# Gated linear attention with a multiplicative FFN: natural feature order, PSUM banks shared 4 + 2, and TensorE in a written order from unit 1 on

## The chip, the cores and the metric

The kernel runs on one core of one Trainium2 chip. The metric is device microseconds for one execution. The engines are TensorE (PE, with its weight loads PEld), VectorE (DVE), ScalarE (ACT), GpSimd (POOL) and SyncE (SP, which issues the DMAs here). All of the work is in float32.

## The reference, cut to what matters

```python
# q, k, v, a_re, a_im: (4 batches, 8 heads, 768 steps, 48)
mag = np.sqrt(a_re * a_re + a_im * a_im)
scale = np.minimum(mag, 0.999) / (mag + 1e-06)
a_re_n, a_im_n = (a_re * scale, a_im * scale)
for t in range(S):                       # complex state S_re, S_im: (B, H, 48, 48)
    new_re = ar * S_re - ai * S_im
    new_im = ar * S_im + ai * S_re
    kv = np.einsum('bhd,bhe->bhde', k[:, :, t], v[:, :, t])
    S_re, S_im = (new_re + kv, new_im)
    y[:, :, t] = np.einsum('bhd,bhde->bhe', q[:, :, t], S_re)
x = y as (3072 tokens, 384 features)
a = x @ w1                               # 384 x 1024
b = x @ w2                               # 384 x 1024
h = a * b @ w3                           # 1024 x 1024
return h @ w_out                         # 1024 x 384
```

## The kernel before, in words

The sequence is cut into 8 units: unit u is one half (384 steps) of one batch, even u the first half and odd u the second. A unit has three chunks of 128 steps. Each unit goes through three parts.

`gates(u)` (L456) works on time-last tiles of 128 x 3 x 384. It turns the gates into running products inside a chunk (gA, L508) and running angles (gZ, L533), and from them into cosine and sine parts of q and k. It is a chain of some fifteen steps, on ScalarE (logarithm, exponential, arctangent, sine, all through L469), VectorE (scans and products, L489 to L554) and GpSimd (three products, L484, L520, L521). Its last steps copy the results by DMA into KL and QL (L563), 96 rows per head. Two sets of these buffers exist (`sides[0]`, `sides[1]`), for even and odd units, so a unit's gates take the buffers that the unit two before it used. `spread_v` (L440), called in it, lays v out into 64 columns per head for the matmuls.

The attention of a chunk has four kinds of matmul. `tp` (L578) transposes the gated k, whose two parts are gR and k, and ScalarE copies it to KT (L579). `sc` (L583) makes the scores of four heads into a bank, and VectorE copies them into A under the causal mask (L584). `y` (L601 to L612) adds V by A and, but for a batch's first chunk, the state T by QL; four column groups of 32 work beside each other, and ScalarE copies the result to xT (L614). `kv` (L619) makes the state's increment, which VectorE adds and scales into T (L625, L626). The last chunk of an odd unit needs no transposes and no state.

The FFN of a unit has eight groups `ffn_ab` (six matmuls m into two banks, L636, then a copy on ScalarE, L640, and a product on VectorE, L641) and three output tiles `ffn_out` (eight matmuls o each, L646; a copy, L649; a store, L651). w3 by w_out is multiplied beforehand, in `fuse` (f, L718).

The weights come as 64-bit floats. `convert` (L659) loads the raw words and turns them into float32 with two ScalarE steps (L670, L671) and four VectorE steps (L672, L674, L675, L676). w1 and w2 are 384 x 1024; each is converted in three tiles of 128 rows.

The features of x stand in an order of their own. Rows 0 to 127 are the first 32 features of heads 0 to 3, rows 128 to 255 the same of heads 4 to 7, rows 256 to 383 the last 16 of all heads. So w1 and w2 are loaded by pieces: four loads of 32 rows for each of the first two tiles, eight loads of 16 rows for the third.

PSUM has eight banks here: two for scores (`ps_s`), one each for tp, y and kv (`ps_1`), three for m, o and f (`ps_m`).

The order of the work is made by a scheduler. The program writes the steps of a unit's attention and of the FFN of the unit before interleaved (`interleave`, L770), with one step of the next unit's gates behind each. From this order as priority and from a cost model the scheduler then makes a fixed stream for each engine: what is ready by its model goes first. On the chip each engine runs its stream in order. `general` (L21) is a fallback that does not run with these inputs; `judge` (L721) decides that by one small matmul near the end.

Of the kernel before, what the change touches and what calls it, by code (L numbers as in the profile page):

```python
# [10 lines left out]
FP = mybir.dt.float32  # L11
# [9 lines left out]
def general(ctx, tc, qt, kt, v, art, ait, w1s, w2s, w3o, ident, out):  # L21
# [83 lines left out]
    def attention(u):  # L105
# [148 lines left out]
        for g in range(2):  # L254
            hd = 2 * hp + g
            for f0, d0, d1 in ((P * (hd // 4) + 32 * (hd % 4), 0, 32), (2 * P + 16 * hd, 32, D)):
                nc.scalar.copy(out=xn_t[b][:, :, f0:f0 + d1 - d0], in_=ys[:, g, :, d0:d1])
# [58 lines left out]
def kernel(  # L316
# [36 lines left out]

# [32 lines left out]
    ps_1 = fast.enter_context(tc.tile_pool(name="ps_1", bufs=1, space=PSUM))  # L386
    ps_m = fast.enter_context(tc.tile_pool(name="ps_m", bufs=3, space=PSUM))
# [26 lines left out]
    g_t, L_t, xT_t, ab_t, T_t, y_t = {}, {}, {}, {}, {}, {}  # L414
# [13 lines left out]
    def load_qkv(u):  # L428
# [6 lines left out]

        vr = one.tile([P, UC, DM], FP, tag="vr", name="vr")
# [131 lines left out]
    def scores(u, c):  # L568
        QL, KL, R, K2 = L_t[u]
        last = u % 2 and c == UC - 1  # L570
        w = slice(c * C, (c + 1) * C)
        A = Ab[(u * UC + c) % 2]
        KT = None if last else two.tile([P, H, 2, D], FP, tag="KT", name="KT")
        for x, src in enumerate((R, K2)):
            if not last:
                tp = ps_1.tile([P, KD, C], FP, tag="tr", name="tp")
                for f in range(KD):
                    nc.tensor.transpose(out=tp[:, f], in_=src[:, f, w], identity=ident)  # L578
                nc.scalar.copy(out=KT[:, :, x], in_=tp.rearrange("p f c -> p (f c)").rearrange("p (d h) -> p h d", h=H))  # L579
            sc = ps_s.tile([P, H // 2, C], FP, tag="sc", name="sc")  # L580
            for j in range(H // 2):
                hd = x * H // 2 + j
                nc.tensor.matmul(out=sc[:, j], lhsT=KL[:, hd, w], rhs=QL[:, hd, w], start=True, stop=True)  # L583
# [248 lines left out]
```

## Time and profile before

| | |
|---|---|
| median of the runs | 711.06 us (704.51, 711.06, 712.73) |
| profiled execution: time | 713.92 us |
| profiled execution: span from first to last instruction | 712.1 us |
| mean granted clock of TensorE | 0.933 |
| busy: TensorE, VectorE, ScalarE, GpSimd | 589.1, 358.4, 256.4, 109.5 us |
| scores of units 1 to 7 begin at | 222.3, 293.2, 367.8, 442.6, 512.5, 587.2, 646.6 us |

In what follows, a row of a timeline has the start, the length, the engine, the line, the operation with its output and inputs, the shape, and in brackets how long the engine had been idle before it and what ended that. Successive instructions of a kind are merged, with their count; one float32 matmul of the program is two instructions. TensorE's busy time counts a matmul from its start to its modelled end, so that a wait between pipelined matmuls can be hidden in it. The clock row of the page has the share of full speed that was granted, in tenths.

### The profile page before, as it was taken

Reading aid. Unit: us, or ns where it says so; the run is one execution under the profiler, and the core shown is the slowest. Engines: PE = TensorE matmul, PEld = TensorE weight load, DVE = VectorE, ACT = ScalarE, POOL = GpSimd, SP = SyncE. Lnnn points to the kernel's source line nnn. Section 1 sums busy time; section 2 is a strip of 40 time slices with the busy share of each in tenths; the row PEclk is TensorE's granted clock in tenths of the full one; section 3 lists DMA queues with packets and bytes.
Section 4 is the critical chain, followed back from the end, with each engine's and each line's share of the span. In section 5 each row is a group of like instructions: output and inputs, shape, how many; then the busy total and the mean of one; then the engine's idle time right before and its main releaser. Section 6 shows DMA issues by size and latency. Waiting matters only on the chain.

```text
span 712.1 us, 8939 instructions
## 1 busy us (share of the span) xinstructions
PE 589.1 (83%) x3514; PEld 382.9 (54%) x3514; DVE 358.4 (50%) x509; ACT 256.4 (36%) x362; POOL 109.5 (15%) x113
## 2 busy tenths in 40 slices
PE   0087994688907899979989899999899999999996
PEld 0044572244506656745667466755675657667553
DVE  2999828667675582358116830774068503103110
ACT  6664514454745533154044502551345101100110
POOL 4355001012122311121012100320122000000000
PEclk9998997699956999999989999999889999999999
DMA  8896975721979504943009700690092009200001
GB/s 238 274 284 191 177 162 124 154 67 33 108 136 115 110 0 114 123 98 100 0 25 123 188 0 1 93 212 30 0 131 37 12 0 117 41 12 13 13 0 37
DMA packets 45044, 65.77 MB, mean 92 GB/s; under 512 B 4288, under 2 KB 43200, under 8 KB 44224
## 3 DMA queue, kind: packets, MB, share of 16 engines
q1 hardware_dynamic: 44992, 65.10, 46.7%
q8 instruction: 29, 0.48, 0.3%
q14 instruction: 23, 0.19, 0.1%
HBM read 41.42 MB, written 4.72 MB: 65 GB/s over the span
## 4 chain that ended last, share of the span: by engine, by line
PE 55%; DVE 20%; ACT 10%; issue 8%; DMA 4%; SPq 2%; DVEq 0%; ACTq 0%
PE m L636 19%; PE o L646 16%; PE sc L583 7%; PE f L718 4%; PE kv L619 3%; DVE gZ L533 3%; DVE gA L508 2%; PE tp L578 2%; ACT gR L469 2%; ACT gZ L469 2%; DMA q<-in_q_dram 2%; DMA raw<-in_w_dram 2%; DVE cf L675 2%; PE y L601 2%; ACT KT L579 2%
## 5 line engine op out<-in xcount | busy, mean ns | idle before, releaser
L636 PE MATMUL m<-xT,w1s 128*128 128x384 f32 x384 | 143.9, 511 | 17.4 <-DVE w1s L676 10.0
L636 PE MATMUL m<-xT,w2s 128*128 128x384 f32 x384 | 138.2, 496 | 9.8 <-DVE w2s L676 8.6
L646 PE MATMUL o<-w3o,ab 128*128 128x384 f32 x384 | 129.7, 494 | 2.7 <-DVE ab L641 2.7
L636 PEld LDWEIGHTS m<-xT,w1s 128*128 128x128 f32 x384 | 73.3, 197 | 73.4 <-DVE w1s L676 12.6
L636 PEld LDWEIGHTS m<-xT,w2s 128*128 128x128 f32 x384 | 73.9, 194 | 65.5 <-DVE w2s L676 11.0
L584 DVE COPY_PREDICATED A<-causal,sc 128x512 f32<-128x512 int32 x48 | 35.1, 739 | 143.4 <-PE sc L583 143.2
L646 PEld LDWEIGHTS o<-w3o,ab 128*128 128x128 f32 x384 | 72.3, 192 | 50.9 <-DVE ab L641 3.3
L718 PE MATMUL f<-wo_s,w3s 128*128 128x384 f32 x128 | 47.9, 538 | 42.9 <-DVE w3s L676 42.9
L641 DVE TENSOR_TENSOR ab<-m,a 128x384 f32<-128x384 f32 x64 | 35.3, 551 | 94.3 <-PE m L636 91.4
L640 ACT COPY a<-m 128x384 f32<-128x384 f32 x64 | 30.3, 474 | 121.2 <-PE m L636 119.6
L718 PEld LDWEIGHTS f<-wo_s,w3s 128*128 128x128 f32 x128 | 26.7, 212 | 62.2 <-DVE w3s L676 43.5
L583 PE MATMUL sc<-QL,KL 96*128 96x128 f32 x384 | 57.6, 317 | 0.0
L583 PEld LDWEIGHTS sc<-QL,KL 96*128 96x128 f32 x384 | 55.0, 229 | 2.9 <-issue 0.8
L484 POOL TENSOR_TENSOR im<-im,gR 128x1152 f32<-128x1152 f32 (+1 forms) x10 | 20.3, 2041 | 229.6 <-ACT gR L469 194.2
L579 ACT COPY KT<-tp 128x384 f32<-128x384 f32 x40 | 19.2, 479 | 95.9 <-PE tp L578 95.5
L614 ACT COPY xT<-y 128x384 f32<-128x384 f32 x24 | 11.4, 475 | 78.5 <-PE y L612 48.8
L520 POOL TENSOR_TENSOR q<-q,gA 128x1152 f32<-128x1152 f32 (+1 forms) x10 | 28.5, 2847 | 61.4 <-DVE gA L508 48.5
L619 PEld LDWEIGHTS kv<-V,KT 128*96 128x96 f32 x320 | 30.1, 165 | 6.1 <-issue 4.4
L578 PE MATMUL tp<-ident,gR 128*128 128x128 f32 x60 | 12.2, 313 | 25.2 <-DVE gR L549 19.6
L619 PE MATMUL kv<-V,KT 128*96 128x64 f32 x320 | 30.8, 248 | 0.9 <-DVE T L625 0.9
L670 ACT ACTIVATE low<-raw 128x1024 int32<-128x1024 uint32 (+1 forms) x18 | 19.7, 1095 | 22.5 <-DVE cf L675 18.4
L521 POOL TENSOR_TENSOR k<-k,gR 128x1152 f32<-128x1152 f32 (+1 forms) x10 | 23.3, 2341 | 23.5 <-DVE gR L518 23.5
(88 smaller groups left out, 670.3 us busy)
## 6 DMA issues: line engine op xcount, KB each, us to landing
raw<-in_w_dram SPq DMA_DIRECT2D x8, 1024.0 KB, 6.0
KL<-gR SPq DMA_DIRECT2D x24, 193.5 KB, 5.1
KL<-k SPq DMA_DIRECT2D x24, 193.5 KB, 7.9
re<-in_a_re_dram SPq DMA_DIRECT2D x24, 192.0 KB, 9.8
im<-in_a_im_dram SPq DMA_DIRECT2D x24, 192.0 KB, 6.5
k<-in_k_dram SPq DMA_DIRECT2D x24, 192.0 KB, 5.3
q<-in_q_dram SPq DMA_DIRECT2D x24, 192.0 KB, 5.0
vr<-in_v_dram SPq DMA_DIRECT2D x8, 576.0 KB, 5.9
```

Source lines behind the costliest of these rows:

```text
L469: chain(nc.scalar.activation(**kw))
L520: nc.gpsimd.tensor_tensor(out=q[:, s], in0=q[:, s], in1=A[:, s], op=OP.mult)
L578: nc.tensor.transpose(out=tp[:, f], in_=src[:, f, w], identity=ident)
L579: nc.scalar.copy(out=KT[:, :, x], in_=tp.rearrange("p f c -> p (f c)").rearrange("p (d h) -> p h d", h=H))
L583: nc.tensor.matmul(out=sc[:, j], lhsT=KL[:, hd, w], rhs=QL[:, hd, w], start=True, stop=True)
L584: nc.vector.copy_predicated(out=A[:, x * H // 2:(x + 1) * H // 2], data=sc, mask=causal.rearrange("p (h t) -> p h t", h=1).to_broadcast([P ...
L619: nc.tensor.matmul(out=kv[:, hd], lhsT=KT[:, hd], rhs=V[:, hd], start=True, stop=True)
L636: nc.tensor.matmul(out=m, lhsT=w[:, f, j * P:(j + 1) * P], rhs=xT_t[u][:, f], start=(f == 0), stop=(f == KD - 1))
L640: nc.scalar.copy(out=a, in_=got[0])
L641: nc.vector.tensor_tensor(out=ab_t[u][:, j], in0=got[1], in1=a, op=OP.mult)
L646: nc.tensor.matmul(out=m, lhsT=ab_t[u][:, f, t * P:(t + 1) * P], rhs=w3o[:, f], start=(f == 0), stop=(f == KF - 1))
L718: nc.tensor.matmul(out=m, lhsT=w3_t[j][:, f], rhs=wo_s[:, f], start=(f == 0), stop=(f == KF - 1))
```

## The change: what it does

Five things are changed at once. The features of x get their natural order (head by head), so w1 and w2 are loaded in three whole tiles each, six loads in place of 32. v is spread by two GpSimd copies per unit in place of nine; of the heads' 64 columns the odd heads now use the last 48. The twelve blocks of 32 features that y is made of are spread over the four column groups as `QUADS`, and the products with V and with T follow each other per block. tp, y and kv share two banks (`ps_v`), and the FFN gets four. And `scores`, `outputs` are cut into `turn`, `scores`, `outputs` and `state`, whose order against the FFN groups is written out in `pieces` and `unit`; from unit 1 on TensorE's stream is exactly that order (`manual_schedule`), while the other engines are still placed by the scheduler.

```diff
-    ps_1 = fast.enter_context(tc.tile_pool(name="ps_1", bufs=1, space=PSUM))
-    ps_m = fast.enter_context(tc.tile_pool(name="ps_m", bufs=3, space=PSUM))
+    ps_v = fast.enter_context(tc.tile_pool(name="ps_v", bufs=2, space=PSUM))
+    ps_m = fast.enter_context(tc.tile_pool(name="ps_m", bufs=4, space=PSUM))
...
-        for c in range(UC):
-            nc.gpsimd.tensor_copy(out=V[:, c, :, 0, 0:D], in_=vr[:, c, :, 0])
-            nc.gpsimd.tensor_copy(out=V[:, c, :, 1, 0:LO], in_=vr[:, c, :, 1, 0:LO])
-            nc.gpsimd.tensor_copy(out=V[:, c, :, 1, D:D + HI], in_=vr[:, c, :, 1, LO:D])
+        for i, e0 in enumerate((0, 64 - D)):
+            nc.gpsimd.tensor_copy(out=V[:, :, :, i, e0:e0 + D], in_=vr[:, :, :, i])
...
+    QUADS = [q for h in range(0, H, 2) for q in ([(h, 0)], [(h, 1), (h + 1, 0)], [(h + 1, 1)])]
...
+        y = ps_v.tile([P, KD, C], FP, tag="v", name="y")
+        lanes = [[] for _ in range(4)]
+        for i, q in enumerate(QUADS):
+            f, j = divmod(i, 4)
+            o = y[32 * j:32 * j + 32, f]
+            got = [(V[:, hd, 32 * e:32 * e + 32], A[:, hd]) for hd, e in q]
+            if not first:
+                got += [(T[:, hd, 32 * e:32 * e + 32], QL[:, hd, w]) for hd, e in q]
+            lanes[j] += [(o, a, b, n == 0, n == len(got) - 1) for n, (a, b) in enumerate(got)]
+        for step in zip(*lanes):
+            for o, a, b, s0, s1 in step:
+                nc.tensor.matmul(out=o, lhsT=a, rhs=b, start=s0, stop=s1)
...
-        got = []
-        for d, w in ((w1s, w1), (w2s, w2)):
-            hs = words(w).rearrange("(h x e) m -> h e x m", x=1, e=D)
-            for f, (h0, h1, e0, e1) in enumerate(((0, 4, 0, LO), (4, 8, 0, LO), (0, H, LO, D))):
-                srcs = [hs[hd, e0:e1] for hd in range(h0, h1)]
-                got.append(lambda d=d, f=f, srcs=srcs: load_weight(d[:, f:f + 1], srcs))
-        return got
+        return [lambda d=d, f=f, src=words(w).rearrange("(f p) m -> p f m", p=P): load_weight(d[:, f:f + 1], src[:, f:f + 1])
+                for d, w in ((w1s, w1), (w2s, w2)) for f in range(KD)]
...
+    def pieces(u):
+
+        sc = [[lambda c=c, x=x: scores(u, c, x) for x in range(2)] for c in range(UC)]
+        tr = [[lambda c=c, x=x: turn(u, c, x) for x in range(2)] for c in range(UC)]
+        kv = [lambda c=c: state(u, c) for c in range(UC)]
+        y = [lambda c=c: outputs(u, c) for c in range(UC)]
+        got = [[tr[0][0]], [tr[0][1]], sc[0], [tr[1][0], kv[0]], [tr[1][1], y[0]], sc[1] + [tr[2][0]], [kv[1], tr[2][1]],
+               [y[1]] + sc[2], [kv[2]], [y[2]]]
+        if u % 2:
+            got[5], got[6], got[8] = sc[1], [kv[1]], []
+        return got
...
+    def unit(u):
         steps = gates(u + 1, False) if u + 1 < NU else iter(())
-        for f in interleave(att, ffn(u - 1) if u else []):
-            f()
-            next(steps, None)
+        rest = ffn(u - 1) if u else []
+        for i, p in enumerate(pieces(u)):
+            for f in rest[i:i + 1] + p:
+                f()
+                next(steps, None)
+        for f in rest[len(pieces(u)):]:
+            f()
+            next(steps, None)
         for _ in steps:
             pass
...
+    unit(0)
+    with tc.manual_schedule(engines={mybir.EngineType.PE}):
+        for u in range(1, NU):
+            unit(u)
+        judge()
+        for f in ffn(NU - 1):
+            f()
```

What the engines' streams make of it is shown at three places. A row there has the line, the operation, the output and inputs with the tile's own number behind the name, the shape and a count. Lines of the changed kernel are its own.

TensorE before, from the FFN of unit 1 into the attention of unit 2 (ab_1294 and o are of FFN(1), sc and y of unit 2):

```order
L646 MATMUL o_1595<-w3o_60,ab_1294 128x384 x8
L646 MATMUL o_1631<-w3o_60,ab_1294 128x384 x8
L619 MATMUL kv_1677<-V0_87,KT_1492 96x64 x8
L646 MATMUL o_1689<-w3o_60,ab_1294 128x384 x7
L583 MATMUL sc_1328<-QL_1215,KL_1214 128x128 x4
L583 MATMUL sc_1339<-QL_1215,KL_1214 128x128 x4
L583 MATMUL sc_1378<-QL_1215,KL_1214 128x128 x4
L583 MATMUL sc_1389<-QL_1215,KL_1214 128x128 x4
L601 MATMUL y_1434<-A0_85,V0_87 32x128 x8
L608 MATMUL y_1434<-A0_85,V0_87 32x128 x8
L583 MATMUL sc_1498<-QL_1215,KL_1214 128x128 x4
```

TensorE now, at the start of unit 3 (m is of FFN(2); tp, sc and kv are of unit 3):

```order
L634 MATMUL m_1650<-xT_1408,w1s_58 128x384 x3
L634 MATMUL m_1654<-xT_1408,w2s_59 128x384 x3
L571 MATMUL tp_1678<-ident_61,gR_1262 128x128 x3
L634 MATMUL m_1686<-xT_1408,w1s_58 128x384 x3
L634 MATMUL m_1690<-xT_1408,w2s_59 128x384 x3
L571 MATMUL tp_1698<-ident_61,k_871 128x128 x3
L634 MATMUL m_1704<-xT_1408,w1s_58 128x384 x3
L634 MATMUL m_1708<-xT_1408,w2s_59 128x384 x3
L581 MATMUL sc_1718<-QL_1443,KL_1442 128x128 x4
L581 MATMUL sc_1735<-QL_1443,KL_1442 128x128 x4
L634 MATMUL m_1743<-xT_1408,w1s_58 128x384 x3
L634 MATMUL m_1747<-xT_1408,w2s_59 128x384 x3
```

The attention stood in one block behind the FFN of the unit before, its pieces behind each other; now each piece has an FFN group before and behind it.

VectorE before, where the gates of unit 1 end (gR_635, k_602), and the rows up to the first masks of unit 1 begin with the gates of unit 2 (gZ_907):

```order
L641 TENSOR_TENSOR ab_893<-m_1142,a_1146 128x384
L549 TENSOR_TENSOR gR_635<-k_602,re_341 128x3x384
L553 TENSOR_TENSOR gA_634<-q_601,re_341 128x1152
L550 TENSOR_TENSOR k_602<-k_602,gZ_636 128x3x384
L554 TENSOR_TENSOR q_601<-q_601,gZ_636 128x1152
L625 TENSOR_TENSOR T_1076<-kv_1067,T_823 96x512
L489 ISA gZ_907,st_tan_98<-im_445 128x1152
```

VectorE now, where the gates of unit 2 end (gR_868, k_588) and the first masks of unit 1 follow (sc_924, sc_941); ab_855 is of FFN(0), T_986 is of unit 1:

```order
L537 TENSOR_TENSOR gZ_869<-gZ_869,re_434 128x1152
L545 TENSOR_TENSOR gR_868<-k_588,re_434 128x3x384
L549 TENSOR_TENSOR gA_867<-q_587,re_434 128x1152
L546 TENSOR_TENSOR k_588<-k_588,gZ_869 128x3x384
L550 TENSOR_TENSOR q_587<-q_587,gZ_869 128x1152
L582 COPY_PREDICATED A1_86<-causal_89,sc_924 128x512
L582 COPY_PREDICATED A1_86<-causal_89,sc_941 128x512
L639 TENSOR_TENSOR ab_855<-m_953,a_957 128x384
L623 TENSOR_TENSOR T_986<-kv_977,T_816 96x512
```

Before, the eighth and last product of FFN(0) (the first row) stood ahead of the end of unit 1's gates, and all of unit 2's gates came after that and ahead of the masks. Now the masks stand behind unit 2's gates as well, and the fourth product of FFN(0) stands behind those masks.

ScalarE before, where unit 2's last copy to xT stands (y_1643; gA_1713 and gZ_1715 are of the gates of unit 4):

```order
L614 COPY xT_1433<-y_1547 128x3x128
L649 COPY ot_1698<-o_1689 128x384
L579 COPY KT_1729<-tp_1730 128x8x48
L469 ACTIVATE gZ_1715<-gA_1713,consts_92 128x1152
L614 COPY xT_1433<-y_1643 128x3x128
```

ScalarE now, at the end of unit 2 (xT_1408 is of unit 2, gZ_1663 and re_1079 are of the gates of unit 4; the last row is the first copy of FFN(2)):

```order
L465 ACTIVATE im_1083<-im_1083 128x1152
L647 COPY ot_1576<-o_1567 128x384
L647 COPY ot_1600<-o_1591 128x384
L465 ACTIVATE re_1079<-gZ_1663 128x1152
L465 ACTIVATE re_1079<-re_1079,consts_92 128x1152
L608 COPY xT_1408<-y_1603 128x3x128
L465 ACTIVATE gZ_1663<-gZ_1663,consts_92 128x1152
L474 ACT_TABLE_LOAD
L638 COPY a_1658<-m_1650 128x384
```

The last copy to xT stood behind an exponential in the first half of unit 4's gates; now it stands behind two activations near their end, the absolute value and the sine that need the running angles.

More of the change, by code (lines that the diff above doesn't have):

```diff
@@ L571, in scores @@
+    def scores(u, c, x):
+        QL, KL = L_t[u][0:2]
         w = slice(c * C, (c + 1) * C)
         A = Ab[(u * UC + c) % 2]
[L573 to L583, printed above, removed]
-            nc.vector.copy_predicated(
-                out=A[:, x * H // 2:(x + 1) * H // 2], data=sc,
-                mask=causal.rearrange("p (h t) -> p h t", h=1).to_broadcast([P, H // 2, C]))
```

94 lines of the change are left out of this document (38 added, 56 removed).

## The prediction

> **What bounds the kernel now.** I read the page first: busy time, the slices and the granted clock.
>
> ```profile
> span 712.1 us, 8939 instructions
> ...
> PE 589.1 (83%) x3514; PEld 382.9 (54%) x3514; DVE 358.4 (50%) x509; ACT 256.4 (36%) x362; POOL 109.5 (15%) x113
> ...
> PE   0087994688907899979989899999899999999996
> ...
> PEclk9998997699956999999989999999889999999999
> ```
>
> TensorE (PE) is busy 83% of the span, the others at most half. Its holes lie in the first third, and there the clock drops too. So I cut the span into stages by windows (columns: length, then busy time of PE, PEld, DVE, ACT, POOL, then clock, DMA share, GB/s).
>
> ```profile
> 111.60:240.70 129.10, 81.61 (x462) 51.15 (x460) 88.71 (x114) 67.02 (x78) 24.15 (x18) 0.78 0.67 116
> 240.70:706.60 465.90, 442.41 (x2654) 288.97 (x2653) 187.90 (x270) 133.12 (x195) 48.96 (x50) 0.97 0.33 58
> 706.60:712.10 5.50, 0.03 (x1) 0.00 (x0) 0.00 (x0) 0.48 (x1) 0.00 (x0) 0.73 0.12 42
> ```
>
> The first stage begins when the attention of unit 0 is done and ends when FFN(1) begins; the second runs to TensorE's last matmul; 5.5 us are a tail that the change leaves alone. A busy PE is not a PE at its pace, so the timeline of TensorE comes next, around the attention of unit 3 (start, length, what, wait before).
>
> ```profile
> 346.11 1.49 PE L619 MATMUL kv<-V,KT 128*96 128x64 f32 x16
> 347.44 15.70 PE L646 MATMUL o<-w3o,ab 128*128 128x384 f32 x48
> 362.98 0.49 PE L578 MATMUL tp<-ident,gR 128*128 128x128 f32 x3
> 364.04 0.55 PE L578 MATMUL tp<-ident,k 128*128 128x128 f32 x3 [0.57 <-ACT KT L579]
> ...
> 367.84 7.06 PE L583 MATMUL sc<-QL,KL 96*128 96x128 f32 x32
> 374.83 0.42 PE L601 MATMUL y<-A,V 128*32 128x128 f32 x8
> 375.07 0.41 PE L604 MATMUL y<-QL,T 96*32 96x128 f32 x8
> ...
> 376.72 2.05 PE L583 MATMUL sc<-QL,KL 96*128 96x128 f32 x16
> 378.70 0.43 PE L601 MATMUL y<-A,V 128*32 128x128 f32 x8
> ...
> 386.39 2.20 PE L636 MATMUL m<-xT,w1s 128*128 128x384 f32 x6 [1.44 <-ACT xT L614]
> 388.43 2.10 PE L636 MATMUL m<-xT,w2s 128*128 128x384 f32 x6
> 390.36 2.10 PE L636 MATMUL m<-xT,w1s 128*128 128x384 f32 x6
> ```
>
> From start to start these rows give the pace of each piece: half an FFN group 1.93 us, so a group 3.87; the three output tiles 15.54; one chunk's scores 1.98 (376.72 to 378.70); one chunk's y with the state 1.89 (374.83 to 376.72); one kv 1.33. Two more pieces, the transposes between two FFN halves and a y without the state:
>
> ```profile
> 267.56 0.49 PE L578 MATMUL tp<-ident,k 128*128 128x128 f32 x3
> 267.88 2.10 PE L636 MATMUL m<-xT,w1s 128*128 128x384 f32 x6
> ...
> 297.10 0.65 PE L601 MATMUL y<-A,V 128*32 128x128 f32 x16
> ...
> 298.11 2.05 PE L583 MATMUL sc<-QL,KL 96*128 96x128 f32 x16
> ```
>
> 0.32 us for three transposes, 1.01 for that y. The 32 instructions at 367.84 took 6.99 us where two chunks' scores take 3.96: 3 us of waiting for the masks count there as busy.
>
> **The change, part by part.** *The work itself.* It stays: the same matmuls per unit, only y alternates V and T in another order over the same four column groups. An even unit (2, 4, 6) is 8 x 3.87 + 15.54 + 3 x 1.98 + 1.01 + 2 x 1.89 + 3 x 1.33 + 6 x 0.32 = 63.1 us, an odd one (3, 5, 7) 30.96 + 15.54 + 5.94 + 3 x 1.89 + 2 x 1.33 + 4 x 0.32 = 62.1. Units 2 to 7 and the last FFN (46.5) are 422.1 us at pace. The window shows 465.9 for the same work: 43.8 us are waits and a clock not yet up, and that is all the new order can win there.
>
> *The fixed order from unit 1 on.* Each attention piece is followed by an FFN group (3.87) or an output tile (5.18) before its result is used. The waits of this kind in the rows (0.57 after a transpose, 1.44 for xT) are shorter than that, so I cost them at nothing; the cover is gone only where VectorE or ScalarE comes to the piece late, and then the piece waits its whole delay. The FFN gets four banks for three, which is two groups; kv, y and the transposes share two, and each finds its bank free one group later. On SP's queue a load of k now stands among the KL and QL copies and waits for transposes; the copies behind it are wanted a unit later, so I count nothing.
>
> What is late next is the gates. They run up to two units ahead, and from unit 2 on a unit's gates can begin only once the transposes of the unit that holds the same buffers are read. In an even unit that is after six groups: 6 x 3.87 + 5 x 0.32 + 2 x 1.98 + 1.33 + 1.01 = 31.1, with the copy 31.6 us in. On ScalarE the last xT copy of the unit now stands behind two of their activations, and FFN of the unit waits for it.
>
> ```profile
> 181.24 1.17 ACT L469 ACTIVATE gR<-gA 128x1152 f32<-128x1152 f32 x1
> ...
> 208.64 1.36 DVE L541 TENSOR_TENSOR gZ<-gZ,re 128x1152 f32<-128x1152 f32 x1
> ...
> 368.43 1.16 ACT L469 ACTIVATE gR<-gA 128x1152 f32<-128x1152 f32 x1
> ...
> 402.61 1.36 DVE L541 TENSOR_TENSOR gZ<-gZ,re 128x1152 f32<-128x1152 f32 x1
> 404.00 1.16 ACT L469 ACTIVATE re<-gZ 128x1152 f32<-128x1152 f32 x1 [7.15 <-DVE gZ L541]
> 405.19 1.25 ACT L469 ACTIVATE re<-re,consts 128x1152 f32<-128x1152 f32 x1
> ```
>
> From gR to the end of gZ it took 28.8 us once and 35.5 the other time. With abs, sine and the copy (about 2.9, an estimate from these rows) xT is there 63.3 to 70.0 us into an even unit that TensorE ends at 63.1: a stall of 0.2 to 6.9 in units 2 and 4. I take 3 each, nearer the short run, since there are few other steps in between: 6 us. In odd units the gates begin at the second transposes, some 13 us sooner, and I count nothing.
>
> *The start: w1 and w2.* 32 loads of 16 or 32 partitions become 6 of 128, and their conversions move on VectorE from behind the attention of unit 0 to behind its first two masks.
>
> ```profile
> 114.54 1.23 DVE L676 SCALAR_TENSOR_TENSOR w1s<-mag,cf 128x1024 f32<-128x1024 f32 x1
> ...
> 119.09 1.23 DVE L676 SCALAR_TENSOR_TENSOR w1s<-mag,cf 128x1024 f32<-128x1024 f32 x1
> ...
> 137.64 1.23 DVE L675 CUSTOM_DVE_ANT_0 cf<-cf,low 128x2048 uint16<-128x2048 uint16 x1 [5.07 <-ACT low L670]
> ...
> 143.52 1.23 DVE L676 SCALAR_TENSOR_TENSOR w2s<-mag,cf 128x1024 f32<-128x1024 f32 x1
> ```
>
> A tile takes 4.55 us. The first masks need a chunk's scores (1.98) and 0.76 for the last mask (a row below). They are ready between 97.8 (scores right behind the last fuse matmul, at 95.1) and 102.9 (if QL of unit 0 lands no sooner than today's first scores begin):
>
> ```profile
> 84.60 10.49 PE L718 MATMUL f<-wo_s,w3s 128*128 128x384 f32 x32
> ...
> 100.16 4.00 PE L583 MATMUL sc<-QL,KL 96*128 96x128 f32 x32
> ```
>
> From 99, nearer the first, six tiles are 27.3, and four masks and states between them 3 more (an estimate at 0.76): 129 to 130; 136 if waits like the 5.07 stay, and no earlier than 128. I take 130, which is 14.8 before today's 144.8.
>
> *Unit 1.* Here the fixed order costs. VectorE runs the gates of unit 1 and all of those of unit 2 before the first masks of unit 1.
>
> ```profile
> 144.78 1.16 ACT L469 ACTIVATE gA<-re 128x1152 f32<-128x1152 f32 x1 [3.39 <-DVE w2s L676]
> ...
> 214.09 0.87 PE L578 MATMUL tp<-ident,gR 128*128 128x128 f32 x3 [19.23 <-DVE gR L549]
> ...
> 217.00 1.35 DVE L554 TENSOR_TENSOR q<-q,gZ 128x1152 f32<-128x1152 f32 x1
> ...
> 224.26 0.76 DVE L584 COPY_PREDICATED A<-causal,sc 128x512 f32<-128x512 int32 x1 [5.91 <-PE sc L583]
> ...
> 240.70 3.42 PE L636 MATMUL m<-xT,w1s 128*128 128x384 f32 x6
> ```
>
> Today both gates take 144.8 to 218.4, 73.6 us. From 130 they end at 203.6; two masks make it 205.1, and the product and the state queued behind them, which frees y's bank, 206.5 (1.4, an estimate at about the masks' length). TensorE by then has done five of FFN(0)'s eight groups and the first scores, and waited at three places. From y on are left 3 x 1.89 + 3 x 3.87 + 2 x 1.98 + 1.33 + 15.54 = 38.1, and 1.3 for a slow start (3.42 at 240.70 against 2.10): unit 1 ends at 245.9, against 240.7 today. So the start gives 14.8, and the order takes that back and 5.2 more: TensorE stands still where it did FFN(0).
>
> *The rest.* V is spread by two copies in place of nine, on GpSimd, busy 15%; it waits for the unit's last y as today, and the work behind it there begins later. The fallback isn't run.
>
> *The sum.* 245.9 + 422.1 + 6 + 2 (a guess for short waits while the third gates run into unit 1) = 676.0; tail 5.5; outside the span 1.8 (the execution's 713.92 less 712.1): 683.3 against 713.92. The median of the runs shown is 711.06, 0.4% lower; scaled by that, 681.
>
> **A rule against the change.** The piece order crosses more often between 128-wide matmuls and the 32-column ones. The rows put both crossings inside 1.89 and 1.33 already. By the Trainium skill, TensorEngine Tiling (Array Packing), Tiling Modes, changing the tiling mode drains TensorE. The page has no price.
>
> **The rivals.**
> 1. *Drains.* Some ten crossings more per unit, each at most the 0.18 us by which the y of 374.83 still ran when 375.07 began: 10 x 7 x 0.18 = 12.6, 694 us. Against it: 0.32 for transposes inside an FFN group.
> 2. *Start not won.* Raw loads or ScalarE keep the conversions at 144.8 (+14.8), and both even units stall 7 (+8): 704. For it: three engines share that stage, 0.67 of the DMA time is taken.
> 3. *Slower: a TensorE that cannot step aside.* In the row at 214.09 it stood 19.23 us before transposes while other work lay behind them. In the Trainium skill, TensorE: Matmul & The Clock Gate, Part 2, matmuls stay in program order and only weight loads are pulled ahead; this trace agrees. If the gates are late in units 2 to 5 as they are in unit 1, 4 x 19.23 = 77 come on top: 758. From 11 us a unit on it is slower than 725. Against it: a unit's gates take 37 us (half of 73.6) in a unit of 63, and are a unit ahead.
> 4. *More gain.* No stall in even units (-6), no short waits (-2), masks at 97.8 (-1), y not held by the state nor slow (-2.7): 669.
>
> **How the numbers follow.** The forecast has 0.55 (its own range 670 to 697: 98 or 136 for the weights, 0.2 or 6.9 for the stalls), rival 4 0.10, drains 0.06, the start 0.18, slower 0.11. The range 664 to 714 leaves out rival 3 and the thin ends. A change under 2% (697 to 725) can hardly be told from none: faster is forecast, rival 4 and most of the drains, 0.69; same 0.20; slower 0.11.
>
> **What would show it.** Right: FFN groups of 3.87 with pieces between and no wait over 1 us from unit 2 on; a TensorE idle before the first transposes of unit 1 and again before its first y, that y near 206; w2s done near 130; busy share near 87%. Wrong: waits on gR, k or QL in units 2 to 5, xT waits over 7 us at the end of units 2 and 4, or groups longer than 4.0 us.

## The result, and the profile after

The changed kernel takes 676.7 us (median of 4 runs, 674.56 to 678.6) against 711.5 (704.51 to 712.73) for the kernel before: a ratio of 0.953, with a 95% interval of 0.946 to 0.960. The prediction was 681 us, in a range from 664 to 714, faster. The profiled execution took 676.36 us, 674.2 of them span, where the sum had said 683.3.

From the page of the changed kernel, its span, TensorE's busy time, and the 40 slices with the granted clock:

```profile
span 674.2 us, 8788 instructions
...
PE 561.5 (83%) x3514; PEld 370.4 (55%) x3514; DVE 363.7 (54%) x509; ACT 258.3 (38%) x362; POOL 104.4 (15%) x57
...
PE   0076993405279999999999999899999999999996
...
PEclk9997998666699999998999999999999999999999
```

The busy share is still 83%. Busy time fell with the span, from 589.1 to 561.5 us for the same 3514 matmul instructions. So most of what was won had not stood in the profile as idle time. Behind the loads of the first slices, the holes are in one place now, slices 7 to 12, and there the clock is at its lowest.

The second stage by windows (columns as in the prediction), from the first FFN group of unit 1 to TensorE's last matmul, and the tail:

```profile
239.40:668.70 429.30, 425.47 (x2685) 280.27 (x2683) 174.03 (x252) 127.15 (x192) 50.35 (x20) 1.00 0.34 62
668.70:674.20 5.50, 0.00 (x0) 0.00 (x0) 0.00 (x0) 0.48 (x1) 0.00 (x0) 0.73 0.12 42
```

That stage took 465.9 us before and takes 429.3 now; the forecast for it was 430.1. Unit 1 ends at 239.4 where it ended at 240.7. Of the 37.9 us that the span lost, 36.6 lie in the steady stage and 1.3 in the start. The granted clock of the stage went from 0.97 to 1.00. The two stages don't hold quite the same work: the rows count 2654 matmul instructions before and 2685 now, since five transposes and a kv of unit 2 had been done ahead of 240.7 before. That is 2.9 us at pace (5 x 0.32 + 1.33), so at equal work the steady stage won some 39 us and the start lost some 2.

TensorE's waits over the whole program, grouped (total us, times, longest):

```profile
PE f L706 <- DVE w3s L672: 43.4, 3, 37.7
PE tp L571 <- issue: 23.9, 1, 23.9
PE y L607 <- DVE A L582: 18.1, 1, 18.1
PE sc L581 <- DMA re<-in_a_re_dram: 12.2, 1, 12.2
PE m L634 <- ACT xT L608: 5.2, 3, 1.9
PE y L607 <- DVE T L623: 2.7, 1, 2.7
PE tp L571 <- ACT KT L572: 1.3, 2, 0.9
```

And where they are, from TensorE's timeline and VectorE's:

```profile
123.79 1.21 DVE L672 SCALAR_TENSOR_TENSOR w2s<-mag,cf 128x1024 f32<-128x1024 f32 x1
...
158.48 0.87 PE L571 MATMUL tp<-ident,gR 128*128 128x128 f32 x3 [23.92 <-issue]
181.32 3.75 PE L581 MATMUL sc<-QL,KL 96*128 96x128 f32 x16 [12.18 <-DMA re<-in_a_re_dram]
...
195.82 1.35 DVE L550 TENSOR_TENSOR q<-q,gZ 128x1152 f32<-128x1152 f32 x1
197.08 1.35 DVE L582 COPY_PREDICATED A<-causal,sc 128x512 f32<-128x512 int32 x2
...
199.52 0.43 PE L607 MATMUL y<-A,V 128*32 128x128 f32 x8 [2.74 <-DVE T L623]
...
304.72 2.94 PE L634 MATMUL m<-xT,w1s 128*128 128x384 f32 x6 [1.90 <-ACT xT L608]
...
434.03 2.20 PE L634 MATMUL m<-xT,w1s 128*128 128x384 f32 x6 [1.90 <-ACT xT L608]
```

The weights are ready at 125.0. Then TensorE stands 23.9 us before unit 1's first transposes, 12.2 before its scores (the row names the load of re; the scores read KL and QL, which go through the same queue), and 2.7 before its first y, which waits until VectorE has run all of unit 2's gates (to 197.17), the two masks and T. All that time, groups of FFN(0) stood behind these pieces; e6 below runs them then. (The 18.1 us are the last y of unit 0, ahead of 125.7: its masks now stand behind the conversions. In the kernel before, TensorE waited there for w1 and w2 instead, 18.6 us in all.) From 239.4 on the only waits are two of 1.90 us at the ends of units 2 and 4.

### The profile page after: what moved, and what is told of

The parts are those of the page before. It is cut to its first block, busy times and chain, and to the rows that moved or that the text cites. A ratio compares the mean times of both kernels' runs of the same rounds, so it can differ in the third digit from the quotient of the medians.

```text
span 674.2 us, 8788 instructions
## 1 busy us (share of the span) xinstructions
PE 561.5 (83%) x3514; PEld 370.4 (55%) x3514; DVE 363.7 (54%) x509; ACT 258.3 (38%) x362; POOL 104.4 (15%) x57
## 4 chain that ended last, share of the span: by engine, by line
PE 68%; DVE 15%; DMA 8%; issue 4%; ACT 3%; SPq 2%; DVEq 0%; ACTq 0%
PE m L634 34%; PE o L644 14%; PE sc L581 6%; PE y L607 5%; PE f L706 4%; PE kv L617 3%; DVE cf L671 2%; DVE cf L670 2%; DVE gZ L529 2%; DMA re<-in_a_re_dram 2%; PE tp L571 2%; DMA QL<-q 2%; DMA raw<-in_w_out_dram 2%; DVE gA L504 1%; DMA KL<-k 1%
## 5 line engine op out<-in xcount | busy, mean ns | idle before, releaser
L634 PE MATMUL m<-xT,w1s 128*128 128x384 f32 x384 | 140.1, 502 | 5.2 <-ACT xT L608 5.2
L581 PE MATMUL sc<-QL,KL 96*128 96x128 f32 x384 | 50.1, 284 | 12.2 <-DMA re<-in_a_re_dram 12.2
L607 PE MATMUL y<-A,V 128*32 128x128 f32 x768 | 41.8, 284 | 20.9 <-DVE A L582 18.1
L581 PEld LDWEIGHTS sc<-QL,KL 96*128 96x128 f32 x384 | 47.7, 197 | 18.5 <-issue 14.7
L607 PEld LDWEIGHTS y<-A,V 128*32 128x32 f32 x768 | 34.4, 113 | 30.4 <-DVE A L582 18.3
L516 POOL TENSOR_TENSOR q<-q,gA 128x1152 f32<-128x1152 f32 (+1 forms) x10 | 25.3, 2530 | 97.9 <-DVE gA L504 72.7
L517 POOL TENSOR_TENSOR k<-k,gR 128x1152 f32<-128x1152 f32 (+1 forms) x10 | 34.5, 3450 | 24.9 <-DVE gR L514 15.0
L607 PE MATMUL y<-QL,T 96*32 96x128 f32 x640 | 36.7, 283 | 0.0
L607 PEld LDWEIGHTS y<-QL,T 96*32 96x32 f32 x640 | 33.0, 115 | 0.1
L465 ACT ACTIVATE gR<-gA 128x1152 f32<-128x1152 f32 (+1 forms) x20 | 19.5, 973 | 33.4 <-DVE gA L504 33.3
```

What stands on the lines that cost most here:

```text
L516: nc.gpsimd.tensor_tensor(out=q[:, s], in0=q[:, s], in1=A[:, s], op=OP.mult)
L517: nc.gpsimd.tensor_tensor(out=k[:, s], in0=k[:, s], in1=r[:, s], op=OP.mult)
L581: nc.tensor.matmul(out=sc[:, j], lhsT=KL[:, x * n + j, w], rhs=QL[:, x * n + j, w], start=True, stop=True)
L607: nc.tensor.matmul(out=o, lhsT=a, rhs=b, start=s0, stop=s1)
L634: nc.tensor.matmul(out=m, lhsT=w[:, f, j * P:(j + 1) * P], rhs=xT_t[u][:, f], start=(f == 0), stop=(f == KD - 1))
```

## The experiments

Two figures are used throughout: where the first FFN group of unit 1 begins (the start), and what is left from there to the end of the span (the stretch). The changed kernel has 239.4 and 434.8 (429.3 and the tail), the kernel before 240.7 and 471.4. Each is read from one execution. A start carries the loads ahead of it too: in the execution of e6 the first scores of unit 0 begin at 91.0, in the changed kernel at 94.3 and in e12 at 95.1. Where the scheduler is free with the old banks, some 3 us of unit 2's work lie ahead of the start.

| kernel | attention | banks | TensorE's order | start | stretch | time, us |
|---|---|---|---|---|---|---|
| before | blocks | old | scheduler | 240.7 | 471.4 | 711.5 |
| e1 | blocks | old | scheduler | | | 700.0 |
| e8 | pieces | old | scheduler | 228.9 | 480.0 | 711.2 |
| e2 | pieces | new | scheduler | 216.5 | 449.9 | 668.7 |
| e3 | pieces | old | fixed | 244.2 | 435.1 | 681.5 |
| e4 | blocks | new | fixed | 251.1 | 435.0 | 688.0 |
| after | pieces | new | fixed | 239.4 | 434.8 | 676.7 |
| e7 | before's blocks and layout | old | fixed from unit 2 | 229.4 | 446.3 | 677.9 |
| e5 | pieces | new | fixed from unit 2 | 216.6 | 437.8 | 656.1 |
| e6 | pieces, FFN(0) first | new | fixed | 210.2 | 439.5 | 654.3 |
| e12 | as e6, last y earlier | new | fixed | 214.5 | 433.4 | 649.6 |

The first theory was that the fixed order makes the gain of the steady stage and that the start is neutral because the same order eats it. Its rivals were the banks and the earlier weights.

### e1: the layout and the loads alone

```diff
-        got = [[tr[0][0]], [tr[0][1]], sc[0], [tr[1][0], kv[0]], [tr[1][1], y[0]], sc[1] + [tr[2][0]], [kv[1], tr[2][1]],
...
+        return [lambda: att(0), lambda: att(1), lambda: out_of(0), lambda: att(2), lambda: out_of(1), lambda: out_of(2)]
...
-    ps_v = fast.enter_context(tc.tile_pool(name="ps_v", bufs=2, space=PSUM))
-    ps_m = fast.enter_context(tc.tile_pool(name="ps_m", bufs=4, space=PSUM))
+    ps_1 = fast.enter_context(tc.tile_pool(name="ps_1", bufs=1, space=PSUM))
+    ps_m = fast.enter_context(tc.tile_pool(name="ps_m", bufs=3, space=PSUM))
...
-    with tc.manual_schedule(engines={mybir.EngineType.PE}):
```

> The changed kernel with the attention in whole blocks as before, the old banks (3 for the FFN, one each for tp, y and kv) and no fixed order: what is left of the change is the natural feature order, the weight loads in whole tiles and the V spread in two copies. Order theory (the 36 us of units 2 to the end come from the written order; the start's 20 us are eaten by the fixed order of unit 1): the weights are ready near 125 us, unit 1 ends some 15 to 20 us earlier than 240.7, units 2 to the end keep the old pace (some 466 us), so 692 to 697 us. Start theory (the gain of the whole change is mostly the earlier weights): 676 to 685 us. Hidden-start theory (the two gate chains bound unit 1, so that earlier weights are worth nothing): 708 to 713 us.

Measured: 699.95 us (696.23 to 707.71), ratio 0.983 (0.976 to 0.990). It lies between the order theory's 692 to 697 and the hidden start's 708 to 713, nearer the first: the earlier weights and the layout are worth about 11 us where the scheduler sets the order. Its profiled execution was 1% above its median, so its stages are left out of the table.

### e2: the same pieces and banks, no fixed order

```diff
-    with tc.manual_schedule(engines={mybir.EngineType.PE}):
-        for u in range(1, NU):
-            unit(u)
+    for u in range(1, NU):
+        unit(u)
```

> The changed kernel without the fixed order of TensorE: the same program order in pieces, the same 4 + 2 banks, but the scheduler places TensorE's work. Order theory: the pace of units 2 to the end falls back most of the way to the old 466 us, 690 to 705 us in all, with TensorE waits of several us in units 2 to 7. Banks theory (4 + 2 banks and the pieces are what makes the steady part faster): 674 to 682 us, as the changed kernel.

Measured: 668.66 us (668.07 to 669.77), ratio 0.943 (0.936 to 0.949). That is below the range of either theory. The order theory as put is wrong: without the fixed order the kernel is 8 us faster still. TensorE's waits in its stretch, grouped:

```profile
PE m L634 <- DVE ab L639: 8.7, 7, 2.9
PE m L634 <- ACT xT L608: 0.9, 2, 0.5
PE y L607 <- DVE A L582: 0.8, 2, 0.5
PE tp L571 <- ACT KT L572: 0.4, 1, 0.4
```

They are 10.8 us, where the changed kernel has 3.8. So the order does two things of opposite sign, and the two figures separate them. In unit 1 it costs 239.4 - 216.5 = 22.9 us: left free, the scheduler puts FFN(0) ahead of the attention that isn't ready. Behind unit 1 it wins 449.9 - 434.8 = 15.1 us.

### e3, e8: the banks, with and without a fixed order

Both kernels have this edit, with banks of their own for y and kv in the same way; e8 has the edit of e2 besides.

```diff
-    ps_v = fast.enter_context(tc.tile_pool(name="ps_v", bufs=2, space=PSUM))
-    ps_m = fast.enter_context(tc.tile_pool(name="ps_m", bufs=4, space=PSUM))
+    ps_1 = fast.enter_context(tc.tile_pool(name="ps_1", bufs=1, space=PSUM))
+    ps_m = fast.enter_context(tc.tile_pool(name="ps_m", bufs=3, space=PSUM))
...
-        tp = ps_v.tile([P, KD, C], FP, tag="v", name="tp")
+        tp = ps_1.tile([P, KD, C], FP, tag="tr", name="tp")
```

> The changed kernel with its fixed order, but with the banks as before: three for the FFN and one each for tp, y and kv. Order theory: 676 to 682 us; a piece's two transposes stand an FFN group apart, so that one bank for them is copied out in time, and an FFN group of 3.87 us leaves its predecessor's two banks time but for the third of three: waits of some tenths of a us. Banks theory: 690 to 711 us, with waits of TensorE for the copies of m of about 1 us in each of the 64 FFN groups.

> The changed kernel's pieces without a fixed order and with the old banks (3 + 3 single ones): what the banks are worth where the scheduler is free. If the 22 us between the free kernel with blocks and old banks (472 us from the first FFN group of unit 1 on) and the free kernel with pieces and new banks (450 us) come from the banks: about 690 us in all. If they come from the pieces: 668 to 674 us.

Measured: e3 681.51 us (679.27 to 681.74), e8 711.19 us (705.77 to 717.42), the latter at a ratio of 1.001 (0.997 to 1.006). Under the fixed order the banks are worth nothing behind unit 1: the stretch is 435.1 against 434.8. The 4.8 us between e3 and the changed kernel lie in the start, and they begin in unit 0, which no kernel here puts in a fixed order. With the old banks its first two masks end at 103.0 in place of 97.1, and the last conversion of w2 comes 5.8 us later (123.79 in the changed kernel). From VectorE's timeline of e3:

```profile
129.62 1.22 DVE L672 SCALAR_TENSOR_TENSOR w2s<-mag,cf 128x1024 f32<-128x1024 f32 x1
```

In e1 and e8, which have the old banks too, this row stands at 131.15 and 129.54; with the new banks it stands at 123.3 to 124.5, and at 120.4 in e6. So some 6 of the 19.8 us by which the weights come sooner (144.8 to 125.0) are owed to the banks. Left to the scheduler the same banks are worth 42.5 us (12.4 in the start, 30.1 in the stretch), more than either theory had allowed. e8's rows show how, from TensorE's timeline and from its waits after unit 1:

```profile
348.89 0.49 PE L571 MATMUL tp<-ident,gR 128*128 128x128 f32 x3
349.95 0.55 PE L571 MATMUL tp<-ident,k 128*128 128x128 f32 x3 [0.57 <-ACT KT L572]
351.07 0.55 PE L571 MATMUL tp<-ident,gR 128*128 128x128 f32 x3 [0.57 <-ACT KT L572]
```

```profile
PE m L634 <- DVE ab L639: 15.2, 8, 3.0
PE tp L571 <- ACT KT L572: 9.2, 16, 0.6
```

Though its text has an FFN group between them, the scheduler puts the transposes together again, and each waits for the one bank; FFN groups wait for VectorE to free a bank. Waits in the stretch are 26.5 us, in e2 10.8. That is 15.7 of the 30.1 us between the two stretches. The windows show the rest as clock: 0.97 against 1.00 over 480 us, some 14 us (an estimate, since the clock has two places).

```profile
228.90:708.90 480.00, 448.31 (x2650) 289.05 (x2650) 186.57 (x265) 133.64 (x195) 42.61 (x23) 0.97 0.29 56
```

```profile
216.50:666.40 449.90, 433.07 (x2678) 283.45 (x2678) 193.33 (x274) 133.48 (x200) 43.47 (x24) 1.00 0.35 64
```

The first row is of e8, the second of e2.

e8 differs from e1 in the pieces alone, and takes 711.2 us against 700.0. So in the scheduler's hands and with the old banks the pieces cost some 11 us, and what e2 wins with these pieces is owed to the banks. Whether the new banks would win as much with the attention in blocks, no run shows.

### e4, e7: whole blocks in a fixed order

e4 has e1's order of pieces with the new banks and the fixed order. e7 is the kernel before with this edit alone:

```diff
+    unit(0)
+    unit(1)
+    with tc.manual_schedule(engines={mybir.EngineType.PE}):
+        for u in range(2, NU):
+            unit(u)
```

> The changed kernel with the attention in whole blocks between FFN groups, as the program before had them in its text, in a fixed order and with the new banks. If it is the fixing that pays, not the cutting into pieces: 677 to 687 us. If the pieces are what hides the copies and masks: each of the 21 blocks left then waits some 1 to 2 us for its copies (two banks for four uses in a row: a ScalarE copy or a mask of 1 to 2 us between), 700 to 720 us.

> The kernel before with nothing changed but that TensorE's order is fixed as the program's text has it from unit 2 on: old features, old banks, old weight loads, attention in whole blocks. Fixing theory (from unit 2 on it is the fixing alone that pays, whatever the banks and the pieces, since three kernels with a fixed order all took 434.8 us from the first FFN group of unit 1 to the end): that group at 240.7 us as before, plus 434.8 to 438 us, so a span of 675 to 679 us and a time of 677 to 682 us. Pieces theory (whole blocks with old banks still wait): 690 to 700 us.

Measured: e4 688.04 us (686.22 to 688.48), e7 677.90 us (676.79 to 679.14), ratios 0.969 (0.962 to 0.976) and 0.954 (0.947 to 0.961). e4's stretch is 435.0, the same to 0.2 us as with pieces. So behind unit 1 cutting the attention up is worth nothing once the order is fixed; e4's 11 us more lie in the start, where its scores wait 22.0 us in place of 12.2. e7 comes to the time of the changed kernel by the fixed order alone. Its time is as forecast, its parts are not, so that the agreement is in part luck: the start is 229.4, 11 us sooner, and the stretch 446.3, 11 us longer. The first row below is of unit 1, the others stand at the beginning of the stretch:

```profile
198.74 3.75 PE L583 MATMUL sc<-QL,KL 96*128 96x128 f32 x16 [6.75 <-DMA QL<-q]
...
229.44 2.20 PE L636 MATMUL m<-xT,w1s 128*128 128x384 f32 x6 [0.75 <-ACT xT L614]
236.25 0.49 PE L583 MATMUL sc<-QL,KL 96*128 96x128 f32 x3 [1.79 <-issue]
253.51 4.21 PE L636 MATMUL m<-xT,w2s 128*128 128x384 f32 x6 [8.05 <-ACT a L640]
```

The start comes sooner because unit 1's scores no longer stand behind transposes of unit 2: in the kernel before, those waited for unit 2's gates until 214.09 and the scores began at 222.3, here at 198.7. A start that comes sooner meets work that isn't ready, 8.05 and 1.79 us of it, and half a group behind it takes 4.21 us for 2.10.

### e5, e6: the order where it wins, not where it costs

e5 leaves unit 1 to the scheduler. e6 keeps it fixed and writes all of FFN(0) ahead of unit 1's attention:

```diff
+        lead = 99 if u == 1 else 0
+        for f in rest[:lead]:
+            f()
+            next(steps, None)
+        rest = rest[lead:]
```

> The changed kernel with TensorE's fixed order from unit 2 on; unit 1 is left to the scheduler, as in the kernel without any fixed order. Two-part theory (the fixed order costs in unit 1, where it makes TensorE wait for inputs while FFN groups are ready, and gains in all units behind it): the FFN of unit 1 begins near 216.5 us as without a fixed order, and the stretch from there to the end takes 434.8 us as with the fixed order, so a span near 651 us and a time of 652 to 656 us. Rival (what unit 1 wins is given back, because the gates of units 2 and 3 come no earlier and the next units wait for them): 664 to 677 us, with waits of tp for gR in units 2 and 3.

> The changed kernel with its fixed order from unit 1 on, but in unit 1 all eleven pieces of unit 0's FFN are written ahead of unit 1's attention. Two-part theory: the FFN of unit 0 runs from about 130 to 178 us where TensorE now waits; the y of unit 1 still start near 199.5 us behind the gates of unit 2 on VectorE, and some 12 us later unit 1 ends, so the FFN of unit 1 begins at 211 to 217 us and the span is 646 to 652 us, the time 648 to 654 us. Rival (gain given back by waits for the gates of units 2 and 3): 664 to 677 us.

Measured: e5 656.06 us (655.17 to 656.91), ratio 0.923 (0.916 to 0.930); e6 654.33 us (651.78 to 656.40), ratio 0.922 (0.915 to 0.929). Both times lie a few tenths above the two-part theory's ranges, and far below the rival's. Forecast for e5 were 216.5 and 434.8, measured are 216.6 and 437.8; for e6 a start of 211 to 217, measured is 210.2, in an execution whose loads came some 3 us early, with a stretch of 439.5. So the fixed order has two separate effects. What it takes in unit 1 is the 23 us that TensorE stood before pieces that weren't ready, and that can be had back while most of the 15 us behind it is kept: the stretches are 3.0 and 4.7 us longer than the changed kernel's, with waits of 6.6 and 7.1 us in place of 3.8.

### e9, e10, e12: what is left of unit 1, and the copy to xT

In e6 TensorE has scores at 181 us, but the masks and the transposes' copy come behind unit 2's gates, at 194.4 and 192.7, as its timeline has them:

```profile
179.04 2.02 PE L581 MATMUL sc<-QL,KL 96*128 96x128 f32 x16 [0.16 <-issue]
...
192.65 0.46 ACT L572 COPY KT<-tp 128x384 f32<-128x384 f32 x1
...
193.16 0.90 PE L571 MATMUL tp<-ident,k 128*128 128x128 f32 x3 [10.44 <-ACT KT L572]
...
194.40 1.36 DVE L582 COPY_PREDICATED A<-causal,sc 128x512 f32<-128x512 int32 x2
```

In e9 they are ordered ahead of the last steps of those gates. e9 also writes unit 1's attention in an order of its own, the scores of chunk 1 ahead of the first y, and all steps of unit 2's gates behind it in the program's text. The edit's core:

```diff
             i0 = ts(out=re[:, s], in0=Z[:, s], scalar1=0.5 / PI, scalar2=ROUND, op0=OP.mult, op1=OP.add)
+            if u == 2:
+                behind(i0, ("sc", 0), ("sc", 1), ("T", 0))
...
             act(out=re[:, s], in_=Z[:, s], func=AF.Abs)
+            if u == 2:
+                behind(chained[-1], ("KT", 0), ("KT", 1), ("xT", 0))
```

e10 is e9, and e12 is e6, with the last y of an even unit one FFN step sooner:

```diff
+        if u % 2 == 0:
+            got[8], got[9] = got[9], got[8]
```

> As the kernel with unit 0's FFN first, and in unit 1 the masks, state updates and copies of the attention are also put ahead of the last steps of unit 2's gates on VectorE and ScalarE, and the scores of chunk 1 ahead of the first y. In the kernel before this one, TensorE had its scores at 181 us, but the masks ran at 194.4, behind the gates of unit 2, and the transposes' copy at 192.65. Theory (what is left of unit 1's waits is this queueing): masks at 184, first y near 187 in place of 196.4, first FFN group of unit 1 at 197 to 200 in place of 210.2, and the stretch from there to the end 435 to 440 us: a span of 633 to 640 us, a time of 636 to 644 us. Rival (the gates of units 2 and 3, now later by some 3 to 5 us while TensorE comes 12 us sooner, make TensorE wait in units 2 and 3, and the gain is given back): 648 to 655 us with waits of tp for gR or of sc for KL and QL.

> As e9, and in even units the last chunk's y stands one FFN step ahead of the last kv instead of behind it, so that its copy to xT has 5 us more before the next FFN. Copy theory (the waits of m for xT, 1.9 us each at the end of the even units, are that copy standing behind the gates' activations on ScalarE): the waits of m for xT go from some 5.5 us to under 1 us, 3 to 5 us below e9. Rival (the y comes earlier but its mask or state is then late): waits of y for A or T in their place, no change from e9.

> The kernel with unit 0's FFN first (654.3 us), and in even units the last y one FFN step ahead of the last kv. Copy theory: the four waits of m for xT (5.5 us in that kernel, 1.9 us the longest) go down to about 1 us, and nothing takes their place: 649 to 651 us. Rival (in the run before, half of the 7.3 us between the two medians was disturbance of the other kernel): 652 to 655 us.

Measured: e9 657.01 us (three runs from 655.74 to 657.42, a fourth of 2083.32), ratio 0.928 (0.919 to 0.936); e10 649.66 us (649.11 to 650.55), ratio 0.917 (0.912 to 0.922); e12 649.59 us (648.00 to 653.15), ratio 0.916 (0.911 to 0.921). e9's start is 201.0, 9 us before e6's, and all of it is given back, and 2 us more than its rival had allowed. Its timeline in unit 2:

```profile
220.67 3.75 PE L599 MATMUL sc<-QL,KL 96*128 96x128 f32 x16 [7.14 <-DMA re<-in_a_re_dram]
237.54 0.55 PE L587 MATMUL tp<-ident,k 128*128 128x128 f32 x3 [2.41 <-ACT KT L588]
240.79 1.93 PE L627 MATMUL y<-A,V 128*32 128x128 f32 x32 [2.70 <-DVE T L643]
```

Unit 2 now waits 7.1 us for its own KL and QL, and 5.1 more for copies and state. The edit also ends unit 2's gates later, at 202.9 against 194.5 in e6 (3.6 of these 8.4 us stand already at the end of unit 1's gates). So the chain of gates sets the time there: TensorE comes sooner and the gates later. The edit of two lines is worth more: the waits of m for xT go from 6.8 us to 1.3 between e9 and e10, and from 5.5 to 0.6 between e6 and e12, and the times fall by 7.3 and 4.7 us. The runs of e6 and e12 overlap by 1.4 us, but their stretches, 439.5 and 433.4, stand apart. e10 and e12 are the fastest kernels found and can't be told from each other, 27 us below the changed one.

### e11: the price of a crossing

A crossing is a place in TensorE's stream where a 32-column matmul (y) and another kind meet. In units 2 to 7 the 8 score matmuls of chunk 2 are laid singly among the y matmuls of chunk 1 (`two` holds its two score tasks, `one` the y):

```diff
+            for g in two:
+                for _ in g:
+                    next(one, None)
...
+        if u > 1:
+            got[7] = [both]
```

> The changed kernel with one thing added: in units 2 to 7 the 8 score matmuls of chunk 2 are laid singly between the first 16 y matmuls of chunk 1 (some 14 more crossings between 128-wide and 32-column matmuls per unit, 84 in all); no other order, wait or work is changed. Drain theory at the price of the rival in the prediction (0.18 us a crossing): 676.7 + 15 = 692 us. Cheap-crossing theory (0.04 us, the difference between the mean score matmul of the free kernel before, 316 ns, and that of the fixed one, 277 ns): 676.7 + 3.4 = 680 us. None: 675 to 678.5 us.

Measured: 690.71 us (688.49 to 691.58). The start is 239.2, as in the changed kernel, and the stretch 450.3: 15.5 us for 84 crossings, 0.185 us each. The waits are 1.6 us shorter than before (2.2 us in the stretch), so a crossing may cost up to 0.20 us. Rows of such a place:

```profile
280.34 0.49 PE L581 MATMUL sc<-QL,KL 96*128 96x128 f32 x2
280.75 0.41 PE L608 MATMUL y<-A,V 128*32 128x128 f32 x4
281.10 0.49 PE L581 MATMUL sc<-QL,KL 96*128 96x128 f32 x2
```

A pair of scores and four y take 0.76 us from start to start (280.34 to 281.10). At pace they would take 0.37 (two sixteenths of 1.98, and four sixty-fourths of 1.89), so two crossings cost 0.39. By the Trainium skill, TensorEngine Tiling (Array Packing), Tiling Modes, a change of the tiling mode drains TensorE; the run agrees that a change costs time, and adds the price. That it is the drain that takes this time, the run doesn't show by itself.

## Why the prediction was right, and where it wasn't

**The slack of the steady stage** carried it, and is confirmed: 422.1 us at pace and 8 of stalls made 430.1, measured 429.3. The reading that a stage's time at pace, not the busy share, tells what there is to win held too, though the 465.9 us were not for the same work: 2.9 us of it lay ahead of 240.7, so the slack was 46.7 us and not 43.8. The 8 us are met in part by luck. The stalls are 3.8 us, no short waits are left, and 3.4 us are matmuls slower than pace; 1.8 of these are the group at 304.72, behind the first stall, which took 5.67 us at a clock of 0.77. What the prediction called waits and a clock not yet up can now be split: the waits went from 23.4 to 3.8 us, the clock from 0.97 to 1.00 over 466 us, which is some 14 (an estimate), and 19.6 + 14 leaves some 3 of the 36.6. One of its readings was wrong: the 3 us by which the scores at 367.84 ran over their pace were no waiting for masks but a low clock, as the last section shows.

**"That is all the new order can win there"** holds for the fixed order, which won most of that slack. What the prediction did not weigh is which part of the new order does it, and what the banks do. The fixed order wins some 36 of the 36.6 us with the old banks (e3) or with blocks (e4), and 25 us with both and the old layout (e7, fixed from unit 2), where work came too early for its inputs. The pieces add nothing to it. The banks are a second remedy for the same waits: without a fixed order they win 30.1 us of the stretch (e8 to e2) and 21.5 against the kernel before; behind unit 1 of a fixed order they win nothing. So the two together gain little over the order alone.

**The fixed order costed at nothing behind unit 1** was right: in e3 and e4 neither bank nor cover missing changes the stretch by more than 0.3 us. **Two stalls of 3 us** were right in place and cause, and measured 1.90 each; e12 takes them away. ScalarE's timeline shows the copy behind the second of the two activations that the prediction named, ahead of TensorE's row at 304.72:

```profile
303.05 1.25 ACT L465 ACTIVATE re<-re,consts 128x1152 f32<-128x1152 f32 x1
304.21 0.46 ACT L608 COPY xT<-y 128x384 f32<-128x384 f32 x1
```

**The start** was right as a mechanism, with its first term too large. The weights were ready at 125.0, not 130, and this row of VectorE's timeline, the second mask of unit 0, shows the first part of it:

```profile
96.33 0.75 DVE L582 COPY_PREDICATED A<-causal,sc 128x512 f32<-128x512 int32 x1 [0.16 <-PE sc L581]
```

The first masks were done at 97.1, where 99 was taken and 97.8 was the lower bound; the six tiles and what lies between them then took 27.9 us, forecast 27.3 + 3. With the old banks the same masks were done at 103.0 (e3), about the upper bound of 102.9: the banks, which had no part in that sum, decide between the two. Both gates took 72.2 us (to 197.17), forecast 73.6; y came at 199.5, forecast 206.5; what was left took 39.9, forecast 39.4. That agreement is in part luck: the 1.3 us for a slow first group at the end didn't come (2.10 us at 239.38), but the first y and the half group behind it took 1.7 us more than at pace. So unit 1 ended 6.5 us sooner than forecast, 5.0 of them from the weights, and this is nearly all of the 6.9 us by which the sum of 683.3 lay above 676.36. That the order takes back what the start gives was forecast at 14.8 + 5.2 = 20.0 us; e2 measures 22.9.

**The rivals.** *Drains* had the price right, 0.18 us (e11: 0.185), and the count wrong. Counted in the two programs' order, y meets other matmuls 42 times before and 50 after: 8 crossings more, not 70, so 1.5 us. *A TensorE that can't step aside* happened in unit 1 alone, as the forecast took it, and never in units 2 to 5; e9 shows how near it was: with the FFN of unit 1 9 us sooner and the gates of unit 2 8 us later it came back in unit 2. *Start not won* didn't happen: the conversions came earlier still. *More gain* came in part: the first masks were as early as it had them and no short waits were left, but both stalls stood, and the first y of unit 1 still waited 2.74 us for the state and ran slowly.

**The busy share near 87%** was wrong: 83%. TensorE's rows at a low clock count as busy, so busy time shrank beside the span.

What stays open: where e4 loses part of its 11 us in the start, and some 5 us of the 15.1 between e2 and the fixed order (waits are 7.0 of them, and 18 crossings more in the stretch at 0.185 make 3.3).

## What to carry to other kernels

Price an engine's stage by its work at pace, since stalls that lower the clock hide in its busy time. A fixed order on one engine protects it from a scheduler that bunches work on too few buffers, but makes it wait wherever an input is late: fix it only from the unit on where the inputs run ahead, and write ready work ahead of work whose inputs are still coming. Where two remedies aim at the same waits, undo each alone before crediting one, and check what sets the time next before pushing further.

## What was not expected of the hardware

**Short waits close together can be followed by half the clock.** In the kernel before, four waits of 0.57 us within 4 us stand ahead of the scores at 367.84, which took 7.06 us for two chunks where each chunk takes 1.98 at pace. The prediction read the difference as waiting for masks. The window over these 7 us, and VectorE's rows in it, show that it is the clock:

```profile
367.80:374.80 7.00, 7.00 (x34) 6.89 (x32) 2.22 (x3) 4.98 (x8) 2.50 (x1) 0.51 0.36 77
```

```profile
371.63 0.75 DVE L584 COPY_PREDICATED A<-causal,sc 128x512 f32<-128x512 int32 x1 [0.96 <-PE sc L583]
373.34 0.72 DVE L584 COPY_PREDICATED A<-causal,sc 128x512 f32<-128x512 int32 x1 [0.96 <-PE sc L583]
```

The clock was 0.51, and VectorE waited for the scores before each mask, so the masks held nothing up. Other places of the same kernel show that such waits alone don't decide it. Over their own length, the scores at 512.48, behind four of them, had 0.56; behind three, those at 442.63 had 0.69 and those at 587.16 had 1.00; behind none, those at 293.23 and 646.58 had 1.00. In the changed kernel the one wait of 1.90 us at 304.72 was followed by 0.77 over 7.3 us, the equal one at 434.03 by 1.00. The Trainium skill, TensorE: Matmul & The Clock Gate, Part 1, has the clock halve after an idle window of about 3.4 us; the clock did halve here, but no single wait ahead of 367.84 was that long. What decides between these places, no run tested.

**A crossing between 128-wide and 32-column matmuls costs 0.185 us** (e11), and it stands in the rows as busy time (442.4 us in the stretch in place of 425.5), not as a wait.
